# Turning centred features with the DMA transpose through DRAM instead of TensorE, in an mLSTM and Fourier-mix kernel

## The chip, the cores and the metric

The kernel runs on one NeuronCore of a Trainium2 chip. The metric is the device time in microseconds (us) of the whole program, and the median of several runs is compared. Profiled executions are looked at for the reasons; the profile's own span is a little shorter than the device time, since it runs from the first to the last instruction.

## The reference

Two blocks follow each other. An mLSTM cell runs over 4 batches, 8 heads, 768 tokens and 40 features a head; its output, laid side by side, is x with 320 features per token. A Fourier mixing block follows:

```python
X = np.fft.fft(np.fft.fft(x, axis=1), axis=2)
u = x + np.real(X)
mu = np.mean(u, axis=-1, keepdims=True)
var = np.mean((u - mu) ** 2, axis=-1, keepdims=True)
un = (u - mu) / np.sqrt(var + 1e-06)
return u + np.maximum(un @ w_ch1, 0.0) @ w_ch2      # 320 -> 1280 -> 320
```

What matters here is the step between u and the first product. TensorE sums over partitions. u is made with tokens on the partitions, and u @ w_ch1 sums over features, so the centred u must be turned until features lie on the partitions.

## The kernel before

All data are fp32. A batch has 768 tokens in six blocks of 128. For each batch b three stages follow each other: the mLSTM in chunks, the mix (the Fourier sums, u, its mean and variance, the turning) and the MLP. The stages of neighbouring batches are interleaved: while the MLP of batch b-1 runs on TensorE, the mLSTM and then the mix of batch b are slipped in between its products.

The order is written by hand. `at(slot, phase, fn, ...)` files a step under a slot number and a phase (EVAC 0, FILL 1, MAIN 2, FILL_PE 3, and decimals between), and `run` emits the steps sorted by that key. Every engine then executes its own instructions strictly in that order, as do the queue of DMAs that SP issues and, where it issues any, ScalarE (ACT). So a step that waits holds up what is filed behind it on its engine.

The mix of batches 1, 2 and 3 begins at slots 54, 83 and 115, their MLPs at slots 63, 95 and 127. One slot is one MLP step. In the mix stage a slot of batch 0's second layer is ten products of 128x320 (L1184), and a slot of a later batch's second layer is ten or five products of 128x160 on each of one or two banks (`mlp_out_pair`, L1240). The six blocks are taken in the order `ORDER` = 0, 5, 1, 4, 2, 3. Their steps are:

- `mix_add` (L940): VectorE (DVE) adds the Fourier part to u and takes the mean and variance of the row (L960 to L966).
- `mix_center` (L968): ACT writes uc, minus the centred row, 384 wide (features 128 to 191 stand in it twice), L974.
- `mix_turn` (L976): three fp32 TensorE transposes of 128x128 into a PSUM bank put (L981).
- `mix_turn_out` (L983): ACT copies put, 128x384, to uT (L986). `uT_bufs[0]` holds the blocks 0, 5, 1, and `uT_bufs[1]` the blocks 4, 2, 3.

The MLP opens with `mlp_sums` (L1104): DVE makes three differences of parts of uT and changes one part of uT in place (L1109). The first of them reads `uT_bufs[1]`, all of whose blocks must be there. `mlp_block` (L1111) then multiplies: its first two products read `uT_bufs[0]` alone, its third reads the part that DVE changed.

Three steps of the mLSTM of the next batch share ACT's order with the mix. `mlstm_exp` (L491) makes the weights W. `halves_between` (L697) copies one element of the PSUM tile ph into `warm` (L699), and the second half of the products into ph (`halves_from_chunk(..., 1)`, L519) waits for that copy. `mlstm_tanh` (L605) follows it. SP issues the loads of that mLSTM (qk, kvt, W, so, Gb), the moves of rows x<-so (L728) and the stores of finished blocks (L1193).

PSUM banks of batches 0 and 1 are dealt out by the string `turn` (L86), one character for each tile asked for; batches 2 and 3 name their banks.

## Time and profile before

| What | Value |
|---|---|
| Median of 3 runs | 391.04 us (389.86 to 391.17) |
| Profiled execution, own time | 390.34 us |
| Its span in the profile | 388.6 us |
| Granted TensorE clock | 1.00 |
| PE, DVE, ACT, POOL busy | 378.2, 276.2, 172.4, 136.7 us |
| DMA, share of 16 engines (queue of SP) | 40.8% |
| Turning: 72 PE transposes | 273 ns each (median) |
| Turning: 24 ACT copies uT<-put | 11.2 us in all, 477 ns each |

PE is the matrix engine, PEld its loading of weights, SPq the queue in which SP issues DMAs. In a timeline the columns are the start and the duration in us, engine, line, operation, output<-input, and in brackets the idle time before the group and who ended it. Matmuls are pipelined: a group's duration overlaps the start of the next group, so the time that a group costs on PE is the distance of its start to the next start.

### The profile page before, as it was taken

What the parts mean: (1) busy time and instruction counts of PE and PEld (TensorE: products, weight loads), DVE (VectorE), ACT (ScalarE), POOL (GpSimd) and SP (SyncE); (2) the same over time, 40 slices, a digit from 0 to 9 for tenths busy, and PEclk for the clock granted to TensorE, in tenths of its full rate; (3) what the DMA queues carried; (4) which work ended last, traced back from release to release, by engine and by line L of the source; (5) the groups of instructions that cost most, each with busy time, mean ns of one, the idle gap of its engine ahead of it and who ended that gap; (6) DMA issues with size and microseconds to landing.
All of it is one profiled execution on the core that took longest, in us unless ns stands there. A gap on an engine that the chain in (4) does not pass through costs nothing.

```text
span 388.6 us, 10587 instructions
## 1 busy us (share of the span) xinstructions
PE 378.2 (97%) x4174; PEld 276.4 (71%) x4174; DVE 276.2 (71%) x671; ACT 172.4 (44%) x481; POOL 136.7 (35%) x237
## 2 busy tenths in 40 slices
PE   8999899999999999999999999999999999999996
PEld 6887455556567677665579989755588995556996
DVE  8699987599698687576975699767655785246652
ACT  6996367377352124564462315454530133545000
POOL 5787415277955433172354133541500000020000
PEclk9999999999999999999999999999999999999999
DMA  7969499678494435538601636400000000000101
GB/s 213 313 195 306 134 236 249 185 217 232 143 229 131 126 98 156 147 87 221 143 11 36 156 101 185 126 19 2 0 2 34 18 19 34 2 0 0 35 34 35
DMA packets 25631, 44.78 MB, mean 115 GB/s; under 512 B 5727, under 2 KB 14766, under 8 KB 25454
## 3 DMA queue, kind: packets, MB, share of 16 engines
q1 hardware_dynamic: 25582, 44.11, 40.8%
q8 instruction: 33, 0.54, 0.6%
q14 instruction: 16, 0.13, 0.1%
HBM read 38.49 MB, written 4.12 MB: 110 GB/s over the span
## 4 chain that ended last, share of the span: by engine, by line
PE 79%; DVE 11%; ACT 4%; DMA 2%; issue 2%; POOL 1%; DVEq 0%; ACTq 0%; POOLq 0%
PE po L1240 20%; PE pm L1121 15%; PE po L1184 8%; PE pm L1059 7%; PE ph L519 4%; PE pm L1126 4%; PE pu L938 4%; PE ps L519 3%; DMA so<-in_o 2%; PE pm L1050 2%; PE put L981 2%; PE pz L907 1%; PE pz L895 1%; DVE h L1130 1%; PE pi L139 1%
## 5 line engine op out<-in xcount | busy, mean ns | idle before, releaser
L1190 DVE SCALAR_TENSOR_TENSOR x<-po,rstd,x 128x160 f32<-128x160 f32 (+1 forms) x69 | 27.1, 394 | 37.7 <-PE po L1240 32.5
L1130 DVE TENSOR_TENSOR h<-h,pm 128x384 f32<-128x384 f32 x60 | 30.5, 549 | 27.1 <-PE pm L1121 12.4
L652 POOL TENSOR_TENSOR C<-C,decB 128x164 f32<-128x164 f32 x30 | 15.9, 529 | 67.9 <-DVE C L667 43.2
L1121 PE MATMUL pm<-uT,w_sb 128*128 128x384 f32 x90 | 37.7, 506 | 1.3 <-DVE uT L1109 0.6
L491 ACT ACTIVATE W<-W,colT 128x64 f32<-128x64 f32 x144 | 37.5, 339 | 1.0 <-DMA W<-M_d 1.0
L1184 PE MATMUL po<-w_sb,h 128*128 128x320 f32 x120 | 34.2, 435 | 0.0
L1005 POOL TENSOR_TENSOR t<-rstd 128x6 f32<-128x6 f32 x12 | 3.3, 272 | 79.9 <-DVE v L999 79.4
L515 POOL TENSOR_SCALAR_AFFINE_SELECT W<-W 64x512 f32<-64x512 f32 x36 | 27.3, 758 | 10.8 <-ACT W L491 5.3
L1059 PE MATMUL pm<-uT,w_sb 128*128 128x384 f32 x80 | 29.2, 500 | 0.1
L1184 PEld LDWEIGHTS po<-w_sb,h 128*128 128x128 f32 x120 | 22.3, 190 | 9.5 <-issue 0.6
L501 POOL TENSOR_TENSOR qg<-qk,Gb 128x512 f32<-128x512 f32 (+1 forms) x21 | 27.1, 1292 | 2.8 <-DMA Gb<-G_d 2.8
L1240 PE MATMUL po<-T,S 128*128 128x160 f32 x180 | 27.8, 301 | 0.3 <-DVE x L1190 0.3
L1240 PEld LDWEIGHTS po<-T,S 128*128 128x128 f32 x180 | 25.5, 190 | 1.7 <-DVE x L1190 0.5
L1121 PEld LDWEIGHTS pm<-uT,w_sb 128*128 128x128 f32 x90 | 15.5, 189 | 15.6 <-DVE h L1130 6.7
L1240 PE MATMUL po<-w_sb,h 128*128 128x160 f32 x180 | 26.3, 300 | 0.0
L1240 PEld LDWEIGHTS po<-w_sb,h 128*128 128x128 f32 x180 | 25.2, 190 | 1.4 <-DVE x L1190 0.3
L986 ACT COPY uT<-put 128x384 f32<-128x384 f32 x24 | 11.2, 477 | 30.1 <-PE put L981 30.1
L507 POOL TENSOR_TENSOR vw<-kvt,colT 128x328 f32<-128x328 f32 x23 | 19.9, 863 | 12.7 <-DMA qk<-in_qkT 10.1
L1177 ACT ACTIVATE h<-h 128x384 f32<-128x384 f32 x45 | 23.1, 520 | 2.0 <-DVE h L1130 2.0
L1126 PE MATMUL pm<-uT,w1t_sb 64*128 64x384 f32 x120 | 23.4, 508 | 0.0
L1059 PEld LDWEIGHTS pm<-uT,w_sb 128*128 128x128 f32 x80 | 14.1, 189 | 9.6 <-issue 1.9
L974 ACT ACTIVATE uc<-x 128x384 f32<-128x384 f32 x24 | 14.4, 613 | 12.6 <-DVE x L966 11.1
(241 smaller groups left out, 841.5 us busy)
## 6 DMA issues: line engine op xcount, KB each, us to landing
kvt<-in_kv SPq DMA_DIRECT2D x24, 336.0 KB
qk<-in_qkT SPq DMA_DIRECT2D x48, 160.0 KB
raw<-in_w SPq DMA_DIRECT2D x10, 640.0 KB
Gb<-G_d SPq DMA_DIRECT2D x36, 128.0 KB
W<-M_d SPq DMA_DIRECT2D x36, 128.0 KB
so<-in_o SPq DMA_DIRECT2D x24, 160.0 KB
out<-x SPq DMA_DIRECT2D x24, 160.0 KB
x<-so SPq DMA_DIRECT2D x9, 140.0 KB
```

Of the source, the lines that this page charges most:

```text
L491: nc.scalar.activation(out=k.W[:, h, :], in_=M, func=AF.Exp, scale=-1.0, bias=colT[:, c, 0, b * H + h:b * H + h + 1])
L501: nc.gpsimd.tensor_tensor(out=k.qg[:, :, t], in0=k.qk[:, 0, :, t], in1=k.Gb[:, :, t], op=OP.mult)
L515: nc.gpsimd.affine_select(out=W, in_=W, compare_op=OP.is_ge, fill=0.0, base=base, pattern=[[0, H], [step, LH]], channel_multiplier=-1)
L519: nc.tensor.matmul(out, w, x, start=start, stop=True, skip_group_check=True)
L1059: nc.tensor.matmul(k.pm[i], w1_sb[:, ch, f0:f0 + L], u[2 * ch], start=(ch == 0 and not ahead), stop=(ch == 1 and ahead), skip_group_check= ...
L1121: nc.tensor.matmul(bank, w, u, start=start, stop=True, skip_group_check=True)
L1126: nc.tensor.matmul(bank, block(w1t_sb, i)[rows], mlp_u(gr, 1)[rows], start=False, stop=True, skip_group_check=True)
L1130: nc.vector.tensor_tensor(out=h, in0=h, in1=bank, op=OP.add)
L1177: nc.scalar.activation(out=h, in_=h, func=AF.Relu, scale=-1.0)
L1184: nc.tensor.matmul(k.po[gr, i], hidden(gr, f)[:, i * L:(i + 1) * L], w2_sb[:, f, :], start=(f == 0), stop=(f == NFF - 1))
L1190: nc.vector.scalar_tensor_tensor(out=u, in0=po, scalar=k.rstd[:, c:c + 1], in1=u, op0=OP.mult, op1=OP.add)
L1240: nc.tensor.matmul(po, a[:, f], w[:, f], start=start and f == 0, stop=f == half - 1, skip_group_check=True)
```

## The change

For batches 1, 2 and 3, the first four blocks of `ORDER` (0, 5, 1, 4) no longer go through TensorE and PSUM. ACT centres them as before, then copies the 384 fp32 words of each row as 768 words of 16 bits, all low halves first and then all high halves, into one of two old buffers (`hT_bufs`, used in turn). ACT itself issues a DMA that stores them in DRAM as 256 rows of 384 words (192 KB). SP issues a DMA transpose that reads those rows and writes uT with features on the partitions, low and high words of a token side by side again. The step that centres is filed one slot after `mix_add`, with the copy and the store right behind it, and the transpose is filed another slot later. The blocks 2 and 3, and all of batch 0, are turned as before.

```diff
+TURNED = 4
...
+    uc_d = dram.tile([B - 1, TURNED, 2 * L, 3 * L], U16, name="uc_d")
...
+    def mix_words(b, c):
+        k = mixes[b]
+        n = ORDER.index(c)
+        words = hT_bufs[n % 2].rearrange("p n t -> p (n t)").bitcast(U16)[:, 0:6 * L].rearrange("p (w m) -> p w m", w=2)
+        of = k.uc[c].rearrange("p two n -> p (two n)").bitcast(U16).rearrange("p (n w) -> p w n", w=2)
+        nc.scalar.copy(out=words, in_=of)
+        nc.scalar.dma_start(out=uc_d[b - 1, n].rearrange("(t w) m -> t w m", w=2), in_=words)
+
+    def mix_words_turn(b, c):
+        n = ORDER.index(c)
+        out = uT_bufs[n // TG].bitcast(U16).rearrange("p ch i t -> p ch (i t)")[:, :, n % TG * 2 * L:(n % TG + 1) * 2 * L]
+        nc.sync.dma_start_transpose(out=out, in_=uc_d[b - 1, n])
...
             at(a, FILL if b < 2 else MAIN - 0.3 if c == 0 else MAIN + 0.5, mix_add, b, c)
+            if b > 0 and c in ORDER[:TURNED]:
+                at(a + 1, FILL + 0.1, mix_center, b, c)
+                at(a + 1, FILL + 0.11, mix_words, b, c)
+                at(a + 2, FILL + 0.8, mix_words_turn, b, c)
+                continue
             at(t, FILL + 0.1, mix_center, b, c)
             at(t, FILL_PE + (5 if b == 0 or c in ORDER[:4] else -0.1), mix_turn, b, c)
```

In the built program PE has twelve groups of three transposes fewer and nothing else of its order changed. ACT has twelve copies to uT fewer, and twelve copies of 128x768 16-bit words and twelve DMA issues more. SP has twelve DMA transposes more. Of each batch's turning steps, `mix_center` moves earlier on ACT: in batch 2 the centring of blocks 5 and 1, their two copies and their two stores now stand ahead of one `halves_between`, where only the centring of block 0 stood there before.

## The prediction

> **What bounds the kernel.** I read the busy times and the chain that ended last, then the groups of the turning step, then the timelines of the three turning stages.

> ```profile
> PE 378.2 (97%) x4174; PEld 276.4 (71%) x4174; DVE 276.2 (71%) x671; ACT 172.4 (44%) x481; POOL 136.7 (35%) x237
> ...
> PE 79%; DVE 11%; ACT 4%; DMA 2%; issue 2%; POOL 1%; DVEq 0%; ACTq 0%; POOLq 0%
> ```

> The reader is to see that PE is idle for 388.6 - 378.2 = 10.4 us in all, and is 79% of the chain. Taking work from PE shortens the kernel where no other engine ends a wait there. DVE is the second bound, ACT has room on average.

> ```profile
> L986 ACT COPY uT<-put 128x384 f32<-128x384 f32 x24 | 11.2, 477 | 30.1 <-PE put L981 30.1
> ...
> L974 ACT ACTIVATE uc<-x 128x384 f32<-128x384 f32 x24 | 14.4, 613 | 12.6 <-DVE x L966 11.1
> ```

> ACT's turning steps wait for PE and DVE, not the reverse. What a turn costs PE is the distance between starts. Batch 1, PE:

> ```profile
> 147.68 0.55 PE L981 MATMUL put<-ident,uc 128*128 128x128 f32 x3
> 148.07 2.86 PE L1184 MATMUL po<-w_sb,h 128*128 128x320 f32 x10
> ...
> 152.58 0.87 PE L981 MATMUL put<-ident,uc 128*128 128x128 f32 x6
> 153.29 2.86 PE L1184 MATMUL po<-w_sb,h 128*128 128x320 f32 x10
> 155.99 0.49 PE L981 MATMUL put<-ident,uc 128*128 128x128 f32 x3
> 156.31 2.86 PE L1184 MATMUL po<-w_sb,h 128*128 128x320 f32 x10
> ```

> These four turns cost 0.39 + 0.71 + 0.32 = 1.42 us, with no idle time beside them. Read alike, batch 2's cost 0.38, 0.39, 0.33, 0.39 = 1.49 and batch 3's 0.32, 0.38, 0.33, 0.32 = 1.35: 4.26 us, 1.1% of the span, is the ceiling of the gain.

> [...] So SP, which runs in order, stands still at each transpose until ACT's store has landed. The trace agrees in kind: SP's waits in order hold up stores for 137.6 us in all without loss. [...]here a 128x128 fp32 one on TensorE shows 273 ns, pipelined to about 0.11 us of PE each, which decides.

> **Part 1: PE and ACT lose the turns.** PE gains at most the 4.26 us above. ACT loses twelve copies of 477 ns, which nobody but the MLP's start waited for.

> **Part 2: copies and stores on ACT.** A copy of 768 words: the fp32 copy of 384 takes 477 ns, the copy of 640 (L414) 723 ns, so 0.96 ns an element gives 0.85 us. Bounds 0.72 (no more than the 640) and 0.95 (twice the 384 one); with the overlap of neighbours I take 0.83. A DMA issued by ACT is not in the trace. SP's plain issues take 0.35 (store) to 0.59 us (load of so); I take 0.45 with 0.1 to 1.0 as bounds. It can't be below nothing, as it is an added instruction in ACT's order. So 1.3 us for each block. Where does it lie on the path? Follow ACT stage by stage.

> Batch 3: no mLSTM is left, ACT idles (6.3 of 26 us busy from 299 to 325). Hidden, at nothing; without that cover, 1.3 us a block. Batch 1: block 0 is centred at 141.23, block 5 after its `mix_add` (142.84); two copies and stores end at 143.5 + 2 x 1.3 = 146.1. The next on ACT is `warm`, which PE releases at 146.83. Hidden with 0.7 us to spare. Blocks 1 and 4 end at 149.4 and 151.5, with no `warm` behind them until 160.73. Batch 2 is the one that pays:

> ```profile
> 228.35 0.15 ACT L699 COPY warm<-ph 1x1 f32<-1x1 f32 x1 [7.73 <-PE ph L519]
> 228.51 0.47 ACT L605 ACTIVATE so<-so 128x320 f32<-128x320 f32 x1
> ```

> ```profile
> 228.22 0.18 DVE L966 BATCH_NORM_AGGREGATE x<-stats 128x2 f32<-128x6 f32 x1
> ```

> ```profile
> 228.86 0.42 PE L519 MATMUL ph<-kvt,W 64*64 64x41 f32 x16
> 229.21 0.55 PE L981 MATMUL put<-ident,uc 128*128 128x128 f32 x3
> 229.59 1.52 PE L1240 MATMUL po<-T,h 128*128 128x160 f32 x10
> ...
> 236.67 1.63 PE L1240 MATMUL po<-T,S 128*128 128x160 f32 x10 [0.30 <-DVE x L1190]
> ```

> Now both centrings stand ahead of this `warm`, the second waits for DVE's end at 228.40, and two copies and stores follow: 228.45 + 0.55 + 2 x 1.3 + 0.15 = 231.8. PE's products at 228.86 need it: PE stalls 3.0 us (2.0 to 4.3 by the bounds), and with PE what is queued behind, L1240's products and DVE's residuals. Then the removed turns pay back: 0.38, 0.39 and 0.33. DVE was busy throughout and PE waited for it at 236.67 (0.30), so part is absorbed: DVE's residual of the 229.59 products moves from 232.35 to about 233.5, and PE's 236.67 to about 238.1, +1.4. The fourth turn gives 0.39 back. Batch 2 nets +1.0 us. The exponentials W, filed behind block 0's store, end at about 223.9, before POOL's mask at 225.50: nothing. `so` (tanh) ends at 232.4, before DVE's use at 233.35.

> **Part 3: the transposes on SP.** Issue: none in the trace; a plain issue is 0.35, I take 0.8 with bounds 0.35 and 2.0. Data: the instruction names tiles of 16 rows by 128 words, so 768 rows of 256 B, 48 for each of 16 engines. In the trace's packet records (medians) 256 B took 18 ns and 80 B took 9 ns. As rows that is 0.9 us; as pieces of 32 B, one for each partition of a tile (6,144, so 384 an engine), 3.5 us[...]. [...]I take 0.9 and keep the others. Landing: the last store is issued at 386.2 and the span ends at 388.6, so 2.4 us bounds the rest of a DMA; I take 1.3 beyond the data.

> The place that decides is batch 1, SP:

> ```profile
> 148.20 1.13 SPq L466 DMA_DIRECT2D W<-M_d  x2
> 152.71 0.37 SPq L1193 DMA_DIRECT2D out<-x  x1
> 153.13 0.43 SPq L484 DMA_DIRECT2D so<-in_o  x1
> 153.66 1.09 SPq L478 DMA_DIRECT2D Gb<-G_d  x2
> 154.84 1.47 SPq L728 DMA_DIRECT2D x<-so  x2
> ```

> Blocks 0 and 5 go in after 149.33, their words landed at 148.3 (146.1 + 2.2): they end before 152.71. Block 1 follows Gb at 154.8, block 4 follows x<-so at 157.1 and lands at 157.1 + 0.8 + 0.9 + 1.3 = 160.1. DVE's first difference starts at 162.01 now and would start at 160.6. In time by 0.5 us, so batch 1 keeps 1.42. The loads behind the transposes move by up to 1.6 us; so of 153.13 is first used at 169.07, and they are filed slots ahead: nothing. In batch 2 SP waits at block 5 until about 232.5 and the loads behind it move by 2 to 3 us, with slots of lead; the MLP starts 13 us later. In batch 3 the words land from 308.8 to 315.2, block 4's turn at about 318, and the MLP needs it at 323: at nothing. There PE and DVE follow each other, the first three turns come through (1.0) and the fourth partly, since block 3's centring (L974, 321.57) holds the last turn: 1.2.

> **Sum.** -1.4 + 1.0 - 1.2 = -1.6 us; I round to -1.5 for lock-step waits between the two issuing queues. On the profiled execution's 390.34 us (span 388.6) that is 388.8; that execution lies 0.7 below the median 391.04, and on the median it is 389.5.

> **Rivals.** (a) Slower: the transposes' data are slow. In batch 1 the queue is one after the other: with 3.5 us each, blocks 0 and 5 end at 157, so and Gb at 158, block 1 at 161.5, block 4 lands at 166.7, 6 us after need, so batch 1 gives +4.7, batch 3 about 0 and batch 2 +1.0: +5.7, 396.7. It decides from about 2.9 us each (+2 in all). [...] For it: the 32-byte pieces[...]. (b) The stall of batch 2 is absorbed and all turns come back: -4.26, 386.8. For it: DVE is busy there anyway; against it: `warm` is in ACT's order. (c) It doesn't do what it says, since the turns were hidden: about 391.0. Against it: PE runs without gaps beside eight of them.

> **Chances.** Forecast 0.43 (own range 388.3 to 392.0, by the bounds of ACT's issue and of SP's), (a) at 3 to 6 us 0.32, (a) worse 0.10, (b) 0.10, (c) 0.05. A measurement here can tell about 0.5%, or 2 us. The forecast case splits 0.08 faster, 0.32 same, 0.03 slower; with the rivals: faster 0.18, same 0.37, slower 0.45. The range drops the worst of (a) and the outermost of (b): 387.2 to 397.5.

> **What would show it.** Right: no put of blocks 0, 5, 1, 4 on PE; a PE gap of about 3 us ahead of the second ph group at slot 89 with ACT's copies before `warm`; `e<-uT` (L1109) in batch 1 waiting for ACT or nothing. Wrong: `e<-uT` or the third L1121 product waiting for a DMA into uT, an SP issue of over 2 us, or no gap in batch 2. The forecast falls if a transpose takes over 2.9 us.

## The result, and the profile after

The change made the kernel slower: 395.77 us median of 20 runs (392.93 to 399.75) against 391.12 us (389.86 to 393.43) in 20 runs of the kernel before, a ratio of 1.0103 (95% interval 1.0081 to 1.0125). The forecast was 389.5 us. The profiled execution of the changed kernel took 397.5 us (span 395.8), that of the kernel before 390.34 (388.6): 7.2 us apart.

Lines are now numbered three to 21 higher: the puts are L997, the ACT copies of put L1002, the sums of uT L1130, the MLP's products L1142 and the pairs L1261. The first view is the page of the changed kernel: busy time, the TensorE clock that was granted in 40 equal slices of the span (9 is 90% or more of full speed), and the shares of the chain that ended last.

```profile
PE 379.0 (96%) x4138; PEld 276.0 (70%) x4138; DVE 276.8 (70%) x671; ACT 177.8 (45%) x481; POOL 138.1 (35%) x237
PEclk9999999999999999799999998999999999999999
PE 78%; DVE 10%; ACT 4%; DMA 3%; issue 2%; POOL 1%; SPq 0%; ACTq 0%; DVEq 0%; POOLq 0%
```

PE has 36 matmuls fewer and is busy 0.8 us longer. That contradiction is the first clue, and the clock row holds the second: two of its slices are below 9, where all 40 are 9 on the page of before. PE also stood still for 395.8 - 379.0 = 16.8 us instead of 10.4.

The two dips follow two new idle stretches. Batch 1, PE's timeline before, and then that of the changed kernel:

```profile
161.28 0.42 PE L519 MATMUL ph<-kvt,W 64*64 64x41 f32 x16
161.63 2.57 PE L1121 MATMUL pm<-uT,w_sb 128*128 128x384 f32 x6
```

```profile
160.60 0.42 PE L522 MATMUL ph<-kvt,W 64*64 64x41 f32 x16
164.47 4.21 PE L1142 MATMUL pm<-uT,w_sb 128*128 128x384 f32 x6 [3.45 <-ACT uT L1002]
168.47 1.46 PE L1142 MATMUL pm<-raw 128*128 128x384 f32 x2
```

PE waits 3.45 us for an ACT copy, and then six products take 4.21 us, which took 2.57 before. Batch 1 began 0.54 us later in this execution (its first pu at 138.70 instead of 138.16), so that much of a difference between two times of batch 1 is no loss. ACT's and SP's timelines say what the copy waited for:

```profile
163.93 0.86 ACT L1002 COPY uT<-put 128x384 f32<-128x384 f32 x2 [3.36 <-DMA uT<-uc_d]
```

```profile
150.90 2.70 SPq L990 DMA_TRANSPOSE uT<-uc_d  x2
...
156.37 1.29 SPq L990 DMA_TRANSPOSE uT<-uc_d  x1
157.75 1.48 SPq L731 DMA_DIRECT2D x<-so  x2
159.28 1.24 SPq L990 DMA_TRANSPOSE uT<-uc_d  x1
```

The transpose of block 4 is issued at 159.28 and landed by 163.93. Behind it stand the copies of blocks 2 and 3, which write other columns of the same tile `uT_bufs[1]`; behind them PE's first product. That product reads `uT_bufs[0]` alone, but its PSUM bank is the one in which block 2's put lay: with four tiles fewer asked for, the string that deals out banks stands elsewhere. DVE's first sum waits for the same copies:

```profile
164.83 0.56 DVE L1130 TENSOR_TENSOR e<-uT 128x384 f32<-128x384 f32 x1 [5.75 <-ACT uT L1002]
```

Batch 2, ACT's timeline and then PE's, same kernel:

```profile
234.06 0.81 ACT L984 COPY h<-uc 128x768 uint16<-128x768 uint16 x1
234.90 0.34 ACTq L985 DMA_DIRECT2D uc_d<-h  x1
235.28 0.83 ACT L984 COPY h<-uc 128x768 uint16<-128x768 uint16 x1 [0.41 <-ACT h L984]
236.14 0.34 ACTq L985 DMA_DIRECT2D uc_d<-h  x1
236.53 0.15 ACT L702 COPY warm<-ph 1x1 f32<-1x1 f32 x1 [0.41 <-ACT h L984]
```

```profile
236.73 0.44 PE L522 MATMUL ph<-kvt,W 64*64 64x41 f32 x16 [2.59 <-ACT warm L702]
237.10 2.16 PE L1261 MATMUL po<-T,h 128*128 128x160 f32 x10
```

This is the stall that was foreseen, 2.59 us against 3.0. What follows was not: ten products take 2.16 us, not the 1.52 of before. The windows view gives the granted clock after each stall (columns: the stretch in us, its length, busy PE, PEld, DVE, ACT, POOL, then clock, DMA share, GB/s):

```profile
158.00:164.50 6.50, 3.05 (x137) 2.58 (x135) 0.55 (x1) 1.16 (x5) 0.00 (x0) 0.88 0.73 173
164.50:170.00 5.50, 5.50 (x9) 3.04 (x10) 3.39 (x7) 1.76 (x7) 1.16 (x2) 0.52 0.62 183
...
237.00:241.50 4.50, 4.50 (x29) 3.49 (x22) 2.52 (x9) 2.99 (x10) 1.16 (x2) 0.62 0.91 256
```

The clock records of the trace give it exactly: 0.5 for 6.83 us from 162.95, and for 3.41 us from 238.05. I count the half clock in windows of 3.41 us, so 6.83 is two. By my estimate from these lengths one window costs up to 1.7 us (half of 3.41), and lowers the mean clock over the span of 395.8 us by 0.0043. Sorted by mean clock, and counted by this estimate, the runs of the changed kernel stand at 392.93 to 394.49 us with 0.995 or 0.996 (one window), at 394.64 to 397.47 with 0.990 or 0.991 (two), at 396.95 to 397.54 with 0.986 or 0.987 (three), and one at 399.75 with 0.982. The profiled execution has three, at 0.986, so it is longer than the median.

To compare executions I cut the span at landmarks of PE: the first pu of each batch (the Fourier sum that opens its mix), the first pm product of batch 2 (which opens its MLP) and the first tail product of each batch (the first that reads `w1t_sb`, some 5 to 7 us into the MLP). The stretch ahead of the first landmark varies between executions and is left out. What does not change between kernels agrees to 0.05 us: the stretch from batch 1's tails to batch 2's first pu is 50.56 us in both profiles.

| Stretch, us | before | after | difference |
|---|---|---|---|
| batch 1's mix: first pu to first tails | 28.09 | 32.64 | +4.55 |
| batch 2's mix: first pu to first pm | 29.76 | 32.45 | +2.69 |
| batch 2's first block: first pm to tails | 6.92 | 7.46 | +0.54 |
| batch 2's tails to batch 3's first pu | 45.10 | 44.62 | -0.48 |
| batch 3's mix: first pu to first tails | 30.07 | 29.41 | -0.66 |

So batch 1 lost 4.55 us, batch 2 2.75 (its three stretches together), and batch 3 gained 0.66.

### The profile page after: what moved, and what is told of

It is laid out like the page before. It is cut to its first block, busy times and chain, and to the rows that moved or that the text cites. A ratio compares the mean times of both kernels' runs of the same rounds, so it can differ in the third digit from the quotient of the medians.

```text
span 395.8 us, 10544 instructions
## 1 busy us (share of the span) xinstructions
PE 379.0 (96%) x4138; PEld 276.0 (70%) x4138; DVE 276.8 (70%) x671; ACT 177.8 (45%) x481; POOL 138.1 (35%) x237
## 4 chain that ended last, share of the span: by engine, by line
PE 78%; DVE 10%; ACT 4%; DMA 3%; issue 2%; POOL 1%; SPq 0%; ACTq 0%; DVEq 0%; POOLq 0%
PE po L1261 21%; PE pm L1142 17%; PE pm L1080 6%; PE po L1205 6%; PE pm L1147 5%; PE ph L522 4%; PE pu L941 4%; PE ps L522 3%; DMA so<-in_o 2%; PE pm L1071 2%; PE pz L910 1%; PE pz L898 1%; DMA uT<-uc_d 1%; PE pi L142 1%; ACT W L494 1%
## 5 line engine op out<-in xcount | busy, mean ns | idle before, releaser
L1151 DVE TENSOR_TENSOR h<-h,pm 128x384 f32<-128x384 f32 x60 | 30.5, 549 | 29.4 <-PE pm L1142 12.6
L1142 PE MATMUL pm<-uT,w_sb 128*128 128x384 f32 x90 | 39.5, 530 | 4.0 <-ACT uT L1002 3.4
L1142 PEld LDWEIGHTS pm<-uT,w_sb 128*128 128x128 f32 x90 | 16.4, 198 | 18.7 <-DVE h L1151 6.4
L1080 PE MATMUL pm<-uT,w_sb 128*128 128x384 f32 x80 | 29.2, 500 | 0.1
L504 POOL TENSOR_TENSOR qg<-qk,Gb 128x512 f32<-128x512 f32 (+1 forms) x21 | 27.9, 1328 | 2.6 <-DMA raw<-in_w 1.6
L1261 PE MATMUL po<-T,S 128*128 128x160 f32 x180 | 27.8, 301 | 0.0
L1261 PEld LDWEIGHTS po<-w_sb,h 128*128 128x128 f32 x180 | 25.2, 190 | 2.0 <-issue 0.6
L1261 PE MATMUL po<-w_sb,h 128*128 128x160 f32 x180 | 26.5, 301 | 0.0
L1261 PEld LDWEIGHTS po<-T,S 128*128 128x128 f32 x180 | 25.6, 190 | 1.2
L1080 PEld LDWEIGHTS pm<-uT,w_sb 128*128 128x128 f32 x80 | 14.1, 189 | 9.6 <-issue 1.9
L522 PE MATMUL ph<-kvt,W 64*64 64x41 f32 x576 | 16.0, 228 | 4.4 <-ACT warm L702 3.4
```

The costliest lines, as they stand in the source:

```text
L504: nc.gpsimd.tensor_tensor(out=k.qg[:, :, t], in0=k.qk[:, 0, :, t], in1=k.Gb[:, :, t], op=OP.mult)
L522: nc.tensor.matmul(out, w, x, start=start, stop=True, skip_group_check=True)
L1080: nc.tensor.matmul(k.pm[i], w1_sb[:, ch, f0:f0 + L], u[2 * ch], start=(ch == 0 and not ahead), stop=(ch == 1 and ahead), skip_group_check= ...
L1142: nc.tensor.matmul(bank, w, u, start=start, stop=True, skip_group_check=True)
L1151: nc.vector.tensor_tensor(out=h, in0=h, in1=bank, op=OP.add)
L1261: nc.tensor.matmul(po, a[:, f], w[:, f], start=start and f == 0, stop=f == half - 1, skip_group_check=True)
```

## The experiments

My theory: two waits, block 4's transpose in batch 1 and ACT's copies ahead of `warm` in batch 2, and after each of them PE at half speed. The rivals: the added DMA load of all batches, spread out (rival 1); the waits alone, with a clock that costs nothing (rival 2); PE's gain never reaching the end (rival 3). The stretches named below are those of the table.

**One batch at a time.** Each of three edits turns the blocks of a single batch by DMA; the first of them is shown.

```diff
-            if b > 0 and c in ORDER[:TURNED]:
+            if b == 1 and c in ORDER[:TURNED]:
```

> Turned by DMA in batch 1 alone. Theory (two waits, each followed by TensorE at half speed): the whole wait of batch 1 stays, 3 to 3.5 us of idle TensorE ahead of the first pm product behind the ACT copy of put, then 3.4 or 6.8 us of granted clock 0.5; median 393 to 395.5, mean clock 0.991 to 0.996, against 391.1 before. Rival 1 (the DMA load of all three batches, a third of the loss each): 392.7. Rival 2 (the wait alone, no clock): about 392.5, clock 1.0.

> Turned by DMA in batch 2 alone. Theory: one idle stretch of 2.5 to 3 us ahead of the second ph group, behind the warm copy on ACT, then 3.4 us of granted clock 0.5 (1.7 us lost), less 1.4 us of TensorE's own work: 392 to 394, mean clock 0.995. Rival 1 (DMA load, a third): 392.7, and no single idle stretch that accounts for it. Rival 2 (wait without the clock): 391.5 to 392.3.

> Turned by DMA in batch 3 alone. Theory: no stall and no loss of clock there; TensorE's removed work shows at the end: 389.9 to 390.7 (0.4 to 1.2 us faster than before), clock 1.0. Rival 1 (DMA load, a third of the loss): 392.7. Rival 3 (the TensorE gain does not reach the end): 391.1.

Measured: batch 1 alone 395.03 us (ratio 1.0082, 1.0057 to 1.0106), batch 2 alone 393.21 (1.005, 1.0024 to 1.0077), batch 3 alone 391.06 (0.9991, 0.9973 to 1.0009), before 391.19. In the profiles batch 1's stretch is +4.89 us, batch 2's mix +2.73, batch 3's mix -0.67, each with all other stretches within 0.2 us of before. These stretches add up to what the whole change shows, and batch 3 alone loses nothing, so rival 1 falls: each loss stays within its own batch. Batch 1 alone has runs of 391.3 and 391.51 us at a mean clock of 1.0 and 0.999, and one of 396.54 at 0.991: the same program loses nearly nothing or 5 us. Batch 3's gain is seen in the profile, and too small for the medians to tell. Why it is 0.67 and not 1.35, the whole of its four turns, stands in the PE timelines, before and with batch 3 alone:

```profile
309.23 1.52 PE L1240 MATMUL po<-T,h 128*128 128x160 f32 x10
310.59 0.74 PE L938 MATMUL pu<-dd_sb,Z 128*128 128x161 f32 x4
```

```profile
310.39 1.52 PE L1261 MATMUL po<-T,h 128*128 128x160 f32 x10
312.04 0.78 PE L941 MATMUL pu<-dd_sb,Z 128*128 128x161 f32 x4
...
323.06 0.55 PE L997 MATMUL put<-ident,uc 128*128 128x128 f32 x3 [0.39 <-ACT uc L977]
```

The put of block 3 waits 0.39 us for its centring, which waits for DVE; and the pu group starts 1.65 us after the ten products, where the same pair was 1.36 apart before: 0.29 more. 1.35 - 0.39 - 0.29 = 0.67. The first wait is DVE's, the second bound; for the second the profile names no one, but DVE's last addition from an earlier pu ended at 311.90, just ahead of the 312.04.

**Batch 1's transposes a slot earlier.**

```diff
-                at(a + 2, FILL + 0.8, mix_words_turn, b, c)
+                at(a + (1 if b == 1 else 2), FILL + 0.8, mix_words_turn, b, c)
```

> The whole change, but batch 1's four transposes are filed one slot earlier on SP (ahead of the loads of qk, kvt and W, and of so and Gb), so that block 4's is issued some 3 us earlier. Same traffic, same ACT work. Theory: the landing of block 4 is no longer last, the idle time ahead of batch 1's first pm product falls from 3.45 us to under 0.6 and its half-clock stretch goes: 391 to 392.8, against 395.8 of the change. Rival 1 (DMA load): 395 to 396. If W or Gb, now later on SP, become last instead: a wait at the ph products of 158 to 160 us takes the place of the one removed, 393 to 395.

Measured: 395.49 us in 4 runs (1.0109, 1.0079 to 1.0138), a miss. The edit moved block 4's transpose from 159.28 only to 158.88 (0.8 us earlier, counted from batch 1's first pu), since the loads that it passed had themselves been pushed back by the other three. It landed by 162.40, 3.5 us after its issue, not 4.65: more of the gain is this faster landing, which the edit did not aim at, than the earlier issue. The wait fell with it:

```profile
162.93 2.48 PE L1142 MATMUL pm<-uT,w_sb 128*128 128x384 f32 x6 [1.49 <-ACT uT L1002]
```

With a wait of 1.49 us the clock stayed at 1.0 there, the six products took 2.48 us, and batch 1's stretch was +0.27 instead of +4.55. A part of what was won went again in batch 2, where the clock after the same 2.59 us of idle time was at half for 6.83 us this time, not 3.41: its mix +3.98. By its stretches this profile is 2.9 us shorter than that of the change, which is one of the longest of its kernel; the medians, 395.49 and 395.77, tell no difference.

**The wait and the clock apart.** Here PE does a product of the MLP some more times into a free PSUM bank while it waits; the result is written over. First with eight, then with five repetitions.

```diff
+            if b == 1 and i == 0:
+                spare = bank("spare", [L, TG * L], 1)
+                for _ in range(8):
+                    product(spare, A[0, 1], mlp_u(0, 2), True)
             if i == 0:
                 begin(0)
```

> The whole change, and in batch 1's wait TensorE does a product of the MLP eight more times into a PSUM bank that is free there (some 3 us of work, its result written over), so that it isn't idle. Theory: the first real pm product still starts at about 164.5 us, since the wait itself stays; but the granted clock does not fall after it, so the six products that took 4.21 us take about 2.5 again and the 6.8 us at half clock go: 2 to 3.5 us less than the change, 392 to 394. Rival (the half clock is not set by the idle stretch but by something in the load or the data): the clock falls as before and the time is 395.8 or more. Rival 2 (the wait is all, the clock costs nothing): no change, 395.8.

> As the run with the product done eight more times in batch 1's wait, with five more times, since eight took 5.43 us and ended 1.4 us after the wait would have. Theory: some 3.4 us of work fill the wait nearly whole; the first real product starts at 164 to 165 us, the granted clock stays at 1.0 in batch 1, and the stretch from batch 1's first pu to its first tails is 2 to 2.5 us shorter than in the change (32.6 us) and 1 to 1.5 shorter than with eight (31.7): 30.2 to 30.7 us. Median 393 to 395. Rival (the clock costs nothing): the stretch stays at 32 us or more.

Measured: eight took 5.43 us, longer than the wait, and the time was 396.55 us in 4 runs (1.0138, 1.0102 to 1.0174), so the run was not what it was meant to be, though its six products took 2.10 us. With five, 394.31 us in 6 runs (1.0097, 1.0067 to 1.0126), and the PE timeline is the one wanted:

```profile
160.07 3.49 PE L1142 MATMUL spare<-uT,w_sb 128*128 128x384 f32 x10
163.68 2.50 PE L1142 MATMUL pm<-uT,w_sb 128*128 128x384 f32 x6
```

The first real product stands where it stood (25.85 us after batch 1's first pu, 25.77 in the change), so the wait is the same; the clock stays at 1.0 and batch 1's stretch is 30.40 us, as expected, instead of 32.64. Of batch 1's 4.55 us, 2.24 are the clock and 2.31 the wait, less what the turns gave. All ten runs of the two kernels have a mean clock of 0.995 or more, one window of half clock at most, where 14 of the 20 of the change had two or more. Rival 2 falls, by the stretch and the clock: the time of 394.31 alone can't be told from that of the change. From 158.0 to 170.0 us its clock was 1.00, where the change had 0.52 from 164.5 to 170.0, and its DMA share was not lower (0.86 and 0.82 in the stretches from 158.0 and from 164.5, against 0.73 and 0.62). So full-size products with a useless result kept the clock up with no less DMA traffic: idleness, not load or data, lowered it here.

**Block 4 of batch 1 by TensorE.**

```diff
-            if b > 0 and c in ORDER[:TURNED]:
+            if b > 0 and c in ORDER[:3 if b == 1 else TURNED]:
```

> In batch 1 only three blocks are turned by DMA, and block 4, the last, by TensorE as before the change; batches 2 and 3 as changed. Theory: no transpose lands last any more, the idle time ahead of the first pm product falls to under 0.5 us and batch 1's half clock goes; batch 1 then gains about 1 us: 5 to 5.5 us less in the profile than the change, median 391 to 393 with batch 2's wait left. Rival 1 (DMA load): 395. If block 1's transpose, now last, lands late too: a wait of 1 to 2 us stays, 393 to 395.

Measured: 392.44 us in 20 runs (1.0042, 1.0022 to 1.0062). In PE's timeline the first product follows without a wait:

```profile
160.65 0.42 PE L522 MATMUL ph<-kvt,W 64*64 64x41 f32 x16
160.99 2.57 PE L1142 MATMUL pm<-uT,w_sb 128*128 128x384 f32 x6
```

Batch 1's stretch is -0.89 us. One transpose of twelve made all of batch 1's loss.

**The deal of PSUM banks.**

```diff
+                at(t, FILL_PE + 5, lambda: b == 1 and next(turn))
```

> The whole change, but the deal of PSUM banks in batch 1 skips one for each turned block, so that the last two put tiles lie in the banks that they had before the change. Theory: TensorE's first two pm products (they read uT0 alone) no longer stand behind ACT's copy of put and run at about 161 us, some 0.7 us of work moved into the wait; the third waits for DVE's sums of uT1 as late as before: 0.3 to 1 us less than the change, 394.8 to 395.5; the idle stretch is cut into one that may be as short as 3 us. If the bank is what makes the wait (not block 4's landing): the whole 3.45 us goes and the time is 391 to 392.

Measured: 395.22 us in 17 runs (1.0085, 1.006 to 1.011), no difference from the change that could be told. In its profile the first two products ran at once, at 162.32, ahead of ACT's copies at 162.95: with the old banks they no longer wait for these copies. But block 4 also happened to land early, 2.9 us after its issue at 160.02 where it took 4.65 in the profile of the change, and batch 1's stretch was +0.46. So the trace shows the tie by the bank, and no run shows what it costs.

**Batch 2's copies behind `warm`.**

```diff
-                at(a + 1, FILL + 0.1, mix_center, b, c)
-                at(a + 1, FILL + 0.11, mix_words, b, c)
+                late = FILL_PE + 0.6 if b == 2 and c in (5, 1) else FILL
+                at(a + 1, late + 0.1, mix_center, b, c)
+                at(a + 1, late + 0.11, mix_words, b, c)
```

> The whole change, but in batch 2 the centering, copy and store of blocks 5 and 1 are filed on ACT behind the warm copy and the tanh of that slot. Theory: the 2.59 us of idle TensorE ahead of the second ph group falls to 0.5 or less and the half clock after it (3.41 us of granted clock 0.5) goes, with batch 1 as it was: 2 to 3.5 us less than the change, 392 to 394, mean clock higher by about 0.004. Rival 1 (DMA load): 395.8. Rival (another ACT or DVE wait takes its place, such as the transposes of batch 2 landing late): 394 to 396.

Measured: 396.15 us in 4 runs (1.0111, 1.0046 to 1.0176), a miss. The stall is gone, and its half clock with it: the second ph group runs straight on, and batch 2's mix is -0.28 us. But 22 us later, in the first block of batch 2's MLP, the timeline of PE in this kernel has a new gap:

```profile
233.86 0.42 PE L522 MATMUL ph<-kvt,W 64*64 64x41 f32 x16
234.21 1.63 PE L1262 MATMUL po<-T,h 128*128 128x160 f32 x10
...
256.51 0.44 PE L522 MATMUL ph<-kvt,W 64*64 64x41 f32 x16 [2.12 <-issue]
256.88 0.91 PE L1143 MATMUL pm<-uT,w_sb 128*128 128x384 f32 x2
257.63 1.38 PE L1143 MATMUL pm<-raw 128*128 128x384 f32 x2
```

"issue" means that PE waited for nothing that the profile shows. The stretch is +3.14 us, with a half-clock window from 257.73. The whole change has the gap too, 1.02 us at 258.47, the +0.54 of the table. The kernel before has none there, nor have the three with one batch alone.

**Both mends together, and batch 1 left out.** The first has two of the edits above: block 4 of batch 1 goes by TensorE, and batch 2's copies stand behind `warm`. The second has the latter edit, with `if b > 1` in place of `if b > 0`.

> Both mends together: block 4 of batch 1 back on TensorE, and in batch 2 the copies and stores of blocks 5 and 1 behind warm. Theory, from the stretches of the profiles so far (batch 1 -0.9 us, batch 2 -0.3, batch 3 -0.7 against before): 1.9 us less than before, 389 to 389.6, mean clock 1.0. If the gap that has no waker in the profile (1 to 2 us at the batch-3 chunk after batch 2's mixing, at the same place in TensorE's instructions in five kernels) comes again: 0.5 to 3 us of it are given back, 389.6 to 392. Rival 1 (DMA load): 394.

> Batch 1 turned by TensorE as before the change, batch 2 with its copies and stores behind warm, batch 3 as changed. Theory: batch 1 as before, batch 2 -0.3 us, batch 3 -0.7: 390 to 390.7 against 391 before, clock 1.0. If the gap without a waker belongs to a place in TensorE's instructions, it moves 12 turns earlier in the program or goes. Rival 1 (DMA load, two batches of three): 394.

Measured: 391.67 us in 22 runs (1.0027, 1.0007 to 1.0047), and 390.42 in 14 runs (0.999, 0.9971 to 1.001) against 391.09. The first has -0.89 in batch 1, -0.15 in batch 2's mix and -0.67 in batch 3, and gives +2.57 back in the gap, which is 1.39 us long here with a half-clock window from 251.40. The second has no such gap and is the best version found: -1.18 us by its stretches, which its median does not tell from no change. (Its profiled execution, 393.4 us, is the longest of the 14, for a wait of 3.82 us ahead of all these stretches.)

**What the gap belongs to.** Counted in the trace, the gap stands after 3,254 matmul records in seven kernels, whatever instruction is there: at the ph group in the whole change, but three products earlier in the kernels with three turned blocks. It ends 1.2 to 1.7 us after a packet of 16 KB on the queue of instruction fetches (in the change the packet ends at 256.81, the gap at 258.47). Kernels with nine or more TensorE products more than the change ahead of that place lack it. So I added small products early in the program, to the kernel with both mends:

```diff
+        for i in range(0 if first else 4):
+            nc.tensor.matmul(pw[:, 0:64], rest[:, 0:L], rest[:, 0:64], start=True, stop=True, skip_group_check=True)
```

> The kernel with both mends (block 4 of batch 1 on TensorE, batch 2's copies behind warm), and besides twelve products of 64 columns into the idle products' PSUM bank at 50 to 58 us, where TensorE has idle time, as many instructions as stand at other places once the turns are gone; nothing else differs. In the five kernels with the gap without a waker it comes at the same number of TensorE instructions (3254 matmul records), a little after the end of an instruction fetch, and kernels with nine or more further TensorE instructions ahead of it don't have it. Theory (TensorE ran out of instructions, and the place decides): the gap of 1.39 us and the half clock after it go, the stretch from batch 2's first pm product to its tails falls from 9.49 us to 6.9, the mean clock is 1.0 in most runs, and the time 389.2 to 390.3 (twelve small products may cost up to 0.5 us of it), against 391.1 before and 391.7 without them. Rival (the gap is a wait for late data, a DMA or POOL): it stays, 391.5 to 392.3.

> Batch 2's copies behind warm, batch 3 as changed, and in batch 1 two blocks turned by DMA (six more TensorE instructions of turns than in the whole change; three turned blocks gave the gap without a waker, none gave no gap). If the gap goes with the place in TensorE's instructions, it is either there, 3 instructions earlier in the program than with three blocks, or gone; gone, theory gives batch 1 -0.6 us, batch 2 -0.3, batch 3 -0.7: 389.2 to 390.2. With the gap: 390.5 to 392. Rival (the gap is a wait for what block 1's transpose or its store delays): gone here, since block 1 is turned by TensorE.

> The same with one block of batch 1 turned by DMA (nine more TensorE instructions of turns than in the whole change). Theory: batch 1 -0.3 us, batch 2 -0.3, batch 3 -0.7 where the gap doesn't come: 389.4 to 390.4; with it 390.7 to 392.3.

Measured: with the small products 395.46 us in 22 runs (1.0086, 1.006 to 1.0111). The time is a miss: the products became 24 matmuls and took 2.2 us of the critical path, which is about what the eight runs at full clock lost (a median of 393.0 against 390.9 before). The other 14 runs have windows of half clock besides, in places that the one profile, itself at full clock, doesn't show. The gap did what was expected of it: gone from its old place (the stretch is 6.34 us, against 9.49), and another one appeared, at an earlier place. PE's timeline of this kernel:

```profile
98.14 0.42 PE L524 MATMUL ph<-kvt,W 64*64 64x41 f32 x10
100.10 0.32 PE L524 MATMUL ph<-kvt,W 64*64 64x41 f32 x6 [1.54 <-issue]
```

Two turned blocks in batch 1 kept the gap at record 3,254 (2.96 us), though block 1's transpose was gone; one turned block had none. So the gap goes with the number of instructions ahead of it, not with the transposes. The times of these two kernels, 394.97 in 15 runs (1.0085, 1.006 to 1.011) and 396.82 in 6 runs (1.0151, 1.0126 to 1.0177), are misses for another reason, on ACT's timeline of the kernel with two blocks:

```profile
157.33 0.48 ACT L1002 COPY uT<-put 128x384 f32<-128x384 f32 x1 [8.49 <-DMA uT<-uc_d]
```

The copy of block 1 writes its own columns of `uT_bufs[0]` and yet waits for the two transposes into the others. With one block, ACT's first copies wait 6.15 us for the transpose in the same way. Mixing both ways of turning in one tile chained ACT, and with it the centrings and PE, to the DMA: batch 1's stretch is +2.07 with two blocks and +5.29 with one.

## Why the prediction was wrong

**The step that failed** is batch 1 in part 3: "lands at 157.1 + 0.8 + 0.9 + 1.3 = 160.1 ... In time by 0.5 us, so batch 1 keeps 1.42". Four terms were off, each too small. Each transpose held SP for 1.21 to 1.34 us (median 1.274), not 0.8, and block 4's is the fourth in SP's order. The loads between them were issued later too: block 4's transpose came at 159.28, not 157.1 (0.54 us of that is the later start of batch 1). From the issue to the landing it took 4.65 us, not 3.0, and the last packet had ended 2.1 us ahead of the landing, where I took 1.3. The data term was right, though it was my estimate from the 256 B packets of before, and that the data go as rows nothing had shown: the trace now has 768 packets of 256 B for each transpose, at a median of 18 ns, which over 16 engines is the 0.9 us. SP did stand at a transpose until ACT's store had landed, at three of the twelve: 0.2 us in batch 2, 8.4 and 1.8 in batch 3, none in batch 1. So rival (a) had the right place and the wrong mechanism: the data were not slow, the issue and the landing were. That its 396.7 us lies near the 395.77 is luck. The margin of 0.5 us was far thinner than the bounds of its own terms; issue at its upper bound of 2.0 alone would have broken it, and it stood at +1.42 in the sum.

**The coupling** was missed. I let only DVE's sum wait for block 4. ACT's copies of blocks 2 and 3 wait for it too, and PE's first product waits for the bank that these copies read. So `e<-uT` did wait for ACT (5.75 us), which the list of signs counted as right, but ACT was itself waiting for the DMA.

**The clock** was missed. I costed a stall at its length, and the profile before, at a mean clock of 1.000, showed no fall of it. In the changed kernel the clock was 0.5 for 6.83 us after the idle 3.45 us of batch 1, and for 3.41 us after the 2.59 of batch 2. Within each execution all changes of the clock lie whole multiples of 3.413 us apart (in the changed kernel at 162.95, 169.78, 238.05 and 241.46: 2, 22 and 23 windows after the first), so these windows can be laid over the timeline.

The clock fell 15 times in the 16 traces before their last products. In 14 of the windows just before a fall PE had stood still for 1.94 to 3.41 us. In the other one (the kernel with both mends) it had for 1.4, and what else ran in it were small products of 41 and 64 columns. No window after which the clock stayed at full speed had more than 1.82. So, as far as these traces go, the idle time within one window counts, not the length of the gap. The boundary at 162.95 split the 3.45 us of batch 1 into 1.94 and 1.51, and the half clock lasted through the second window too. The 2.59 us of batch 2 left 1.98 us or more in one window in all seven profiles that have them, and the clock fell. A wait of 2.35 us early in the kernel with batch 3 alone was split into 1.74 and 0.61, and the clock stayed. So the same stall can cost two windows, one, or none: of the twelve runs with batch 2 alone, five kept a mean clock of 1.0.

**Batch 2** was right in its mechanism: the stall was 2.59 us, with 3.0 forecast. The +1.0 is what it costs without the clock: the five runs of batch 2 alone with a mean clock of 1.0 have a median of 392.21 us, 1.1 more than the 37 runs of before with 0.999 or 1.0 (391.09).

**ACT's terms** were right: a copy took 0.83 us, as taken, an issue 0.34 to 0.38 (0.45 taken). Batch 1's `warm` waited for PE (1.27 and 1.98 us), not for the copies, and batch 2's exponentials ended at 229.08, ahead of POOL's mask at 230.59.

**Batch 3** had the right sign; -1.2 measured -0.66, since a pu came late as well as the put of block 3, which alone I had seen.

**The chances.** Slower had the largest share, 0.45, and the range held the time, but the likeliest case, the forecast, did not come. My range of the forecast case ended at 392.0, because each unknown term was bounded alone, and not the point at which several of them end together behind one wait.

**Open** is why the landing of the same transpose takes 2.9 to 4.7 us in different executions. The semaphore events of the traces show where the time goes. Each landing has sixteen arrivals there. Of block 4's in the changed kernel fifteen came by 162.22, 2.94 us after the issue, and the last at 163.91; a packet of 16 KB on the queue of instruction fetches was running meanwhile (161.46 to 162.58). Of the 141 transposes whose arrivals are all on record, eight have the last one 1.4 to 1.8 us behind the fifteenth, and in all eight such a packet was running when the fifteenth came; of the other 133 that holds for nine. So the fetches are suspect, but no run moved them alone. For the same reason it is open whether the gap is TensorE short of instructions: the place and the fetch packet speak for it.

## What to carry over

A transfer that moves work off TensorE must land with a margin that covers the issue times of all transfers ahead of it in its queue, as measured (1.21 to 1.34 us for each transpose here), and the spread of its landing (2.9 to 4.7 us for the same transpose); the half microsecond of this forecast was none. A stall of TensorE that left 1.94 us or more of idle time within one window of 3.41 us (once 1.4 was enough) was followed in these traces by one or two windows of half clock, on top of its length, by my estimate up to 1.7 us for each (the two of batch 1 cost 2.24 together); whether it was changed from run to run (five of the twelve runs with batch 2 alone kept a mean clock of 1.0), with the place of the windows. Keep the pieces that come by DMA in a tile of their own: a copy into other columns of the same tile waited 8.49 us for the DMA here.
